# Masked attention with a two-layer network behind it: ten late hidden chunks computed as 2x2 blocks with seven block products

## The chip, the cores and the metric

The kernel runs on one core of a Trainium2 chip. Its engines are TensorE (PE; its weight loads are listed as PEld), VectorE (DVE), ScalarE (ACT), GpSimd (POOL) and SyncE (SP, which here issues all DMAs). The metric is device time in microseconds of one launch.

## The reference

Attention over 8 batches, 8 heads, 576 tokens and head size 64, in which only scores within `tau` of the row's maximum count, and then two dense layers on the 4608 tokens (512 features, 2048 hidden units):

```
scores = scale * q @ k^T
scores = where(scores >= max - tau, scores, -1e9)
x = softmax(scores) @ v            # (4608, 512) over all heads
h = x @ w_in                       # (4608, 2048)
g = max(h, 0) + alpha * min(h, 0)
out = g @ w_out                    # (4608, 512)
```

q, k and v are float32. The weights arrive as 64-bit floating point words and are decoded on the chip. Every float32 matrix operand is split into a high and a low part in the matmul format fp32r, and a product is the sum of three matmuls: high by high, high by low, low by high.

## The kernel before

The hidden units are 16 chunks of 128 (`fc`). The attention works on 32 pairs of heads, in cycles of nine units per pair; its finished outputs go to DRAM (`xs`, features by tokens). The first seven chunks (`F1 = 7`, the early chunks) are worked off as filler between the attention's matmuls: for groups of 256 tokens (`G1`), layer one (`pha`, L210) and layer two (`acca`, L246), and the sum over the early chunks is stored to DRAM as `part`. `Mlp.cycle` decides by a budget of TensorE time how much filler a cycle gets, and a group of tokens counts as ready only when its batch has left the attention. What is left of the early chunks when the attention ends is done behind it, under the names `phj` and `accj` with 256 columns.

Then come nine late chunks in two rounds, four and five chunks, each over all nine groups of 512 tokens (`G2`): x is loaded and split (`xhj` on ScalarE, `xlj` on GpSimd, L835 and L836), layer one takes 12 matmuls of 512 columns per chunk and group, VectorE makes the prelu (L228, L229), ScalarE and GpSimd split it (`gj`, L237 and L240), layer two takes three matmuls of 512 columns per chunk and block of 128 tokens (L246), and VectorE adds the stored partial sum (`pinj`, L988). Gates never leave the core. The weights of the late chunks are decoded piece by piece (128x512 words, class `Split64`: two operations on ScalarE, then on VectorE L137 clamp, L140 shift, L145 sign, L150 power, L156 rest) beside the matmuls of the round ahead.

Within each engine the instructions run in the order in which the program was written. `at_cycle(c, f)` puts a step into that order at a place counted in cycles; behind the attention a cycle is a place in the program, not a time. A tile whose tag has one buffer can be written again only when the last reader of its former content has finished.

## Time and profile before

| | us |
|---|---|
| median of 3 runs (lowest to highest) | 1376.98 (1376.14 to 1378.34) |
| span of the profiled execution | 1374.2 |
| TensorE busy | 1332.0 |
| VectorE busy | 989.5 |
| ScalarE busy | 843.4 |
| GpSimd busy | 825.4 |

The profiled execution's own time is known as its span, from the first to the last instruction; the three runs are other executions and lie 1.9 to 4.1 us above it. The last attention pair ends at about 833 us, the matmuls of the late chunks fill 931.6 to 1370.6 us, and the stretch between holds what is left of the early chunks. A row of an instruction group gives line, engine, operation, output and inputs, shapes and count, then busy time in us and the mean duration of one in ns, then idle time ahead of it and what ended that. A row of the timeline gives the start, the duration and the instruction.

### The profile page before, as it was taken

To read this page: it belongs to the slowest core of one execution; us is meant where nothing else is said; L and a number is where in the kernel's file an instruction comes from. 1 tells how busy PE (TensorE), PEld (TensorE's weight loads), DVE (VectorE), ACT (ScalarE), POOL (GpSimd) and SP (SyncE) were. 2 spreads that over 40 slices of the span, in tenths; PEclk is the share of its full clock that TensorE was granted. 3 is DMA by queue.
4 is the path that set the end of the run, shared out by engine and by line. 5 is a ranking of instruction groups with operands and counts; after the bars stand their busy time and mean duration, and the time that the engine had idled before them with its cause. 6 is when DMAs were issued, how large, how long until landed. Compare 5 with 4: busy or idle time off the path is not lost.

```text
span 1374.2 us, 24020 instructions
## 1 busy us (share of the span) xinstructions
PE 1332.0 (97%) x8116; PEld 1178.4 (86%) x8116; DVE 989.5 (72%) x1970; ACT 843.4 (61%) x1915; POOL 825.4 (60%) x949
## 2 busy tenths in 40 slices
PE   5988899999999999999999999999999999999998
PEld 4556789999999999999999998898888888888887
DVE  6999988889889889888888883873655644333432
ACT  6888888888888888888888873442323322211110
POOL 4886676576676666666666654884656554433431
PEclk9999999999999999999999999999999999999999
DMA  8643634644544545445445313445556352343222
GB/s 253 175 145 104 184 103 119 167 125 125 160 122 134 148 126 144 136 126 150 136 132 145 115 50 110 131 131 169 167 170 200 122 184 92 109 150 110 93 77 77
DMA packets 115179, 186.06 MB, mean 135 GB/s; under 512 B 18320, under 2 KB 49328, under 8 KB 115056
## 3 DMA queue, kind: packets, MB, share of 16 engines
q1 hardware_dynamic: 115056, 184.52, 45.0%
q8 instruction: 65, 1.06, 0.3%
q14 instruction: 58, 0.48, 0.1%
HBM read 104.41 MB, written 37.90 MB: 104 GB/s over the span
## 4 chain that ended last, share of the span: by engine, by line
PE 86%; ACT 5%; DVE 4%; issue 2%; POOL 2%; DMA 2%; SPq 0%; POOLq 0%; DVEq 0%; ACTq 0%
PE accj L246 19%; PE phj L210 18%; PE s L423 11%; PE av L570 11%; PE acca L246 9%; PE pha L210 9%; PE t L467 7%; PE tk L483 1%; DVE p L458 1%; DVE nmx L438 1%; DMA wri<-in_moe_w_in_dram 1%; ACT xb L583 1%; ACT p L446 1%; ACT xa L581 1%; ACT xh L196 1%
## 5 line engine op out<-in xcount | busy, mean ns | idle before, releaser
L240 POOL TENSOR_TENSOR gj<-ptj,gj 128x512 fp32r<-128x512 f32 (+1 forms) x109 | 129.2, 1187 | 237.2 <-ACT gj L237 236.5
L237 ACT ACTIVATE gj<-ptj 128x512 fp32r<-128x512 f32 (+1 forms) x109 | 62.9, 577 | 338.1 <-DVE ptj L229 338.0
L438 DVE TENSOR_REDUCE nmx<-s 128x1 f32<-128x576 f32 x288 | 217.2, 754 | 71.5 <-PE s L423 68.0
L246 PE MATMUL accj<-wo,gj 128*128 128x512 f32 x1140 | 262.4, 389 | 0.5 <-POOL gj L240 0.5
L246 PEld LDWEIGHTS accj<-wo,gj 128*128 128x128 f32 x1140 | 213.7, 188 | 45.3 <-POOL gj L240 1.0
L210 PE MATMUL phj<-xhj,wi 128*128 128x512 f32 (+1 forms) x816 | 232.7, 366 | 0.0
L458 DVE SCALAR_TENSOR_TENSOR p<-s,thr,p 128x576 f32<-128x576 f32 x256 | 206.9, 808 | 2.8 <-ACT thr L451 2.4
L446 ACT ACTIVATE p<-s,nmx 128x576 f32<-128x576 f32 x256 | 190.2, 743 | 8.2 <-DVE nmx L438 7.7
L246 PE MATMUL acca<-wo,ga 128*128 128x512 f32 x588 | 185.9, 422 | 1.6 <-POOL ga L240 0.8
L423 PE MATMUL s<-kh,qst 128*128 128x288 f32 x640 | 142.4, 313 | 33.6 <-DVE p L458 19.1
L210 PEld LDWEIGHTS phj<-xhj,wi 128*128 128x128 f32 x816 | 147.4, 188 | 25.4
L228 DVE TENSOR_SCALAR ptj<-phj,alpha_sb 128x512 f32<-128x512 f32 (+1 forms) x109 | 74.3, 681 | 124.1 <-PE phj L210 120.2
L210 PE MATMUL pha<-xh,wi 128*128 128x256 f32 x784 | 156.8, 283 | 0.2 <-ACT pra L223 0.2
L467 PE MATMUL t<-ident,p 128*128 128x128 f32 x1024 | 154.7, 274 | 0.0
L210 PE MATMUL phj<-xlj,wi 128*128 128x512 f32 (+1 forms) x408 | 149.8, 367 | 1.1 <-POOL xlj L836 0.9
L423 PEld LDWEIGHTS s<-kh,qst 128*128 128x128 f32 x640 | 101.4, 193 | 57.6 <-issue 25.1
L988 DVE TENSOR_TENSOR obj<-accj,pinj 128x512 f32<-128x512 f32 x72 | 49.8, 692 | 139.5 <-PE accj L246 118.5
L423 PE MATMUL s<-kl,qst 128*128 128x288 f32 x640 | 133.7, 299 | 0.0
L210 PEld LDWEIGHTS pha<-xh,wi 128*128 128x128 f32 x784 | 127.9, 190 | 4.5 <-ACT pra L223 1.5
L467 PEld LDWEIGHTS t<-ident,p 128*128 128x128 f32 x1024 | 126.5, 141 | 0.1
L233 POOL TENSOR_TENSOR pta<-pta,pra 128x256 f32<-128x256 f32 x94 | 69.4, 738 | 74.2 <-ACT pra L223 71.6
L246 PEld LDWEIGHTS acca<-wo,ga 128*128 128x128 f32 x588 | 102.0, 191 | 13.7 <-POOL ga L240 1.3
(130 smaller groups left out, 2867.3 us busy)
## 6 DMA issues: line engine op xcount, KB each, us to landing
pinj<-part SPq DMA_DIRECT2D x72, 256.0 KB
kr<-in_k_dram SPq DMA_DIRECT2D x31, 320.0 KB
rb<-rvd SPq DMA_DIRECT2D x64, 144.0 KB
xs<-xa SPq DMA_DIRECT2D x32, 288.0 KB
part<-obj SPq DMA_DIRECT2D x36, 256.0 KB
out_dram<-obj SPq DMA_DIRECT2D x36, 256.0 KB
vr<-in_v_dram SPq DMA_DIRECT2D x28, 320.0 KB
...
```

The source lines that it names most:

```text
L210: nc.tensor.matmul(ph[:, :n], w[:, c, :], xx[:, c, :n], start=(c == 0 and ti == 0), stop=(c == NCC - 1 and ti == 2),)
L228: nc.vector.tensor_scalar(t[:, :n], ph[:, :n], 0.0, alpha_sb[:, fc : fc + 1], op0=ALU.min, op1=ALU.mult)
L233: nc.gpsimd.tensor_tensor(t[:, :n], t[:, :n], r[:, :n], op=ALU.add)
L237: nc.scalar.activation(g[:, 0, :n], t[:, :n], AF.Copy)
L240: nc.gpsimd.tensor_tensor(g[:, 1, :n], t[:, :n], f(g[:, 0, :n]), op=ALU.subtract)
L246: nc.tensor.matmul(acc[:m, :], gg[:, g, o : o + m], w, start=(first and ti == 0), stop=(last and ti == 2))
L423: nc.tensor.matmul(ps[:, h, :288], w, kk[:, a + h * 288 : a + (h + 1) * 288], start=(ki == 0 and i == 0), stop=(ki == 1 and i == n - 1),)
L438: nc.vector.tensor_reduce(self.nmx[:, j : j + 1], self.S[u][0][:, :, :288], axis=AX.XY, op=ALU.max, negate=True)
L446: nc.scalar.activation(pj, ps[:, :, :288], AF.Exp, bias=nmx[:, j : j + 1], scale=1.0)
L458: nc.vector.scalar_tensor_tensor(pj, ps[:, :, :288], thr[:, j : j + 1], pj, op0=ALU.is_ge, op1=ALU.mult, accum_out=self.sm[:, c : c + 1])
L467: nc.tensor.transpose(tb[:, c, :], pt[:, j, j * D + c * P : j * D + (c + 1) * P], ident)
L570: nc.tensor.matmul(pa[:m, :n], w, x, start=(part == 0 and c == 0), stop=(part == z.parts[-1] and c == NKC))
```

## The change

The early chunks are six (`F1 = 6`), the late ones ten. The ten late chunks form five pairs. Both layers of a pair are computed on 2x2 blocks: a block product of eight becomes a set of seven, numbered 1 to 7, whose operands are sums and differences of blocks; the products of a set accumulate in three PSUM banks (`X` takes 1, 6, 5 and 3, `W` 7 and 4, `Y` 2).

- **Stage A**, the whole first layer of the late chunks: 6 blocks (`s`) of 768 tokens by 5 pairs of chunks, 30 units (`u`). A product is 6 matmuls of 384 columns. For each block x is loaded in four parts (`xr`), four sums are made (`xt` and in place) and seven operands are split (`xh`, `xl`, 128x768) by GpSimd, in the first block by VectorE in part. Behind the products, ScalarE copies banks (`c1`, `c7`, `c6`), VectorE and GpSimd add and make the prelu, and the gates go to DRAM (`gd`).
- **Stage B**, the whole second layer: 9 steps (`s`) of 512 tokens. A product is 30 matmuls of 256 columns. The gates are loaded again (`gr`), summed on VectorE (`gt` and in place), and split into `gh` (ScalarE) and `gl` (VectorE for products 7 and 5, GpSimd for the others), 128x1280 each; these lie in three slots, `r % 3`. VectorE adds the banks to the loaded `part` (`pin`), which is stored as the output.
- **Weights**: the ten pieces of `w_in` are decoded, summed and split (`wa`) in the stretch behind the attention, those of `w_out` decoded during stage A (`wo32`), and summed and split in its last block (`wb`).

The diff, cut to its core (the two rounds that go, `decode_part`, `load_pins` and the loop over `jobs` with `parts2`, are left out, and so are loads and pool bookkeeping):

```diff
 S = 576
 NKC = 4
-F1 = 7
+F1 = 6
 G1 = 256
+H1 = 384
 G2 = 512
 
 
...
+    NP = len(fcs2) // 2
+    NJ = 2 * NP
+    NA = NT // (2 * H1) * NP
+    NB = NT // G2
+    H2 = G2 // 2
+    ORDER = ((0, 1), (1, 5), (0, 7), (0, 2), (1, 3), (0, 6), (0, 4))
+    TURN = ((1, 5), (0, 1), (1, 3), (0, 7), (0, 2), (0, 6), (0, 4))
+    LAST = ((0, 1), (1, 5), (0, 7), (1, 3), (0, 6), (0, 2), (0, 5), (0, 4), (0, 3))
+    BANK = {1: "X", 6: "X", 5: "X", 3: "X", 7: "W", 4: "W", 2: "Y"}
+    USE = (1, 7, 2, 6, 4, 5, 3)
+    gd = [dram.tile([2, NP, P, H1], F32, name=f"gd{h}") for h in range(NT // H1)]
+
...
+    def split_hi(dst, src):
+        nc.scalar.activation(dst, src, AF.Copy)
+
+    def split_lo(eng, dst, src, hi):
+        eng.tensor_tensor(dst, src, f(hi), op=ALU.subtract)
...
+        def word_piece(io, fc):
+            src = (src_i if io == "i" else src_o)(fc)
+            return Split64(mem.ws, ("w0", 2), mem.ws, ("w1", 2), ENG2[(fc + (io == "o")) % 2], *src)
+
...
+            def temps():
+                for n in (7, 6):
+                    st[n] = mem.ws.tile([P, m], F32, tag=f"sum{n}", name=f"sum{n}_{pr}", bufs=1)
+                st[5], st[3] = blk(1, 0), blk(0, 1)
+                st[1], st[2], st[4] = blk(0, 0), blk(0, 1), blk(1, 1)
+                tt = nc.vector.tensor_tensor
+                tt(st[7], st[1], st[5], op=ALU.subtract)
+                tt(st[6], st[4], st[7], op=ALU.subtract)
+
+            def hi(n):
+                wsum[pr, n] = mem.wa.tile([P, 2, m], F32R, tag=f"wa{pr}_{n}", name=f"wa{pr}_{n}")
+                split_hi(wsum[pr, n][:, 0], st[n])
+
+            def lo(n, eng):
+                split_lo(eng, wsum[pr, n][:, 1], st[n], wsum[pr, n][:, 0])
+
+            def later_sums():
+                tt = nc.vector.tensor_tensor
+                tt(st[5], st[5], st[4], op=ALU.add)
+                tt(st[3], st[2], st[6], op=ALU.subtract)
+
+            at_cycle(c, temps)
...
+        def first_weights(c0, step):
+            for n, fc in enumerate(fcs2):
+                w = word_piece("i", fc)
+                c = c0 + step * n
+                at_cycle(c + 6, start_w32, fc)
+                word_at(c, w, None, c - 3)
...
+        p1.close()
+        mem.xr = pool(2, "xraw", "left")
+        mem.br = pool(3, "br", "right")
+        mem.pa = pool(4, "pa", "right")
+
+        start = {}
+        steps = []
+        c = i + 1
+        for n in range(NA + NB + 1):
+            for lag, prod in {NA: TURN, NA + NB - 1: LAST, NA + NB: ()}.get(n, ORDER):
+                u = n - lag
+                if 0 <= u < NA + NB:
+                    start[u, prod] = c
...
+        def x_at(s):
+            u = s * NP
+            st = {}
+            need = {n: start[u, n] for n in USE}
+            first = s == 0
+
+            def load():
...
+                        nc.sync.dma_start(r[:, :, t - t0 : t - t0 + m], src)
+                        t += m
+
+            tt = (nc.vector if first else nc.gpsimd).tensor_tensor
+
+            def temp(n):
+                st[n] = mem.xr.tile([P, 2, H1], F32, tag="xt", name=f"xt{s}_{n}", bufs=2)
+                return st[n]
+
...
+            def hi(n):
+                xop[s, n] = tuple(
+                    mem.pa.tile([P, 2, H1], F32R, tag=t, name=f"{t}{s}_{n}", bufs=7) for t in ("xh", "xl")
+                )
+                split_hi(xop[s, n][0], st[src(n)])
+
+            def lo(n):
+                split_lo(nc.vector if first and n in (7, 6) else nc.gpsimd, xop[s, n][1], st[src(n)], xop[s, n][0])
+
+            if first:
+                at = lambda c, fn, *a: fn(*a)
+            else:
+                at = at_cycle
+            at(need[1] - 20, load)
+            for n in USE:
+                c = need[n] - 6
+                fn = {7: sub7, 6: add6, 4: sub4, 5: sub5}.get(n)
+                if fn:
+                    at(c - 2, fn)
+                at(c, hi, n)
+                at(c + 1, lo, n)
+
+        x_at(0)
+        for put in puts:
+            put()
+        left[5].close()
+        ps_3 = left[5].enter_context(tc.tile_pool(name="ps_3", bufs=1, space=PSUM, reuse_waits="tile"))
+        for s in range(1, NA // NP):
...
+        def psum(u, prod):
+            b = BANK[prod]
+            fresh = prod in (1, 7, 2)
+            if fresh:
+                bank[u, b] = ps_3.tile([P, 512], F32, tag=b, name=f"p{b}{u}", bufs=3 if b == "X" else 2)
+            return bank[u, b], fresh
+
+        def product_a(u, prod):
+            s, pr = divmod(u, NP)
+            ph, fresh = psum(u, prod)
+            w = wsum[pr, prod]
+            xh, xl = xop[s, prod]
+            for c in range(2):
+                wh, wl = (w[:, k, c * P : (c + 1) * P] for k in range(2))
+                for ti, (a, x) in enumerate(((wh, xh), (wh, xl), (wl, xh))):
+                    nc.tensor.matmul(
+                        ph[:, :H1],
+                        a,
+                        x[:, c],
...
+        def after_a(u, prod):
+            s, pr = divmod(u, NP)
+            ph = bank[u, BANK[prod]][:, :H1]
+            if prod in (1, 7, 6):
+                t = sv[u, prod] = mem.br.tile([P, H1], F32, tag=f"c{prod}", name=f"c{prod}_{u}", bufs=2)
...
+            al = alpha_sb[:, fc : fc + 1]
+            t = mem.br.tile([P, H1], F32, tag="ct", name=f"ct{prod}_{u}", bufs=2)
+            if of is None:
+                g = mem.br.tile([P, H1], F32, tag="cr", name=f"cr{u}", bufs=1)
+                nc.vector.tensor_scalar(t, ph, 0.0, al, op0=ALU.min, op1=ALU.mult)
+                nc.scalar.activation(g, ph, AF.Relu)
+                nc.gpsimd.tensor_tensor(g, g, t, op=ALU.add)
+            else:
+                g = sv.pop((u, of))
+                nc.vector.tensor_tensor(g, ph, g, op=ALU.add)
+                nc.vector.tensor_scalar(t, g, 0.0, al, op0=ALU.min, op1=ALU.mult)
+                nc.vector.scalar_tensor_tensor(g, g, 0.0, t, op0=ALU.max, op1=ALU.add)
+            nc.sync.dma_start(gd[2 * s + k][r, pr], g)
+
+
...
+        for n in range(NJ):
+            c = begin + 8 + 12 * n
+            fc = fcs2[n]
+            word_at(c, word_piece("o", fc), wo32[:, n // 2, n % 2], c - 4)
+
+        bsum, gop, pin = {}, {}, {}
...
+        def gates_at(s):
+            u = NA + s
+            need = {n: start[u, n] for n in USE}
+            use = sorted(USE, key=need.get)
...
+            def temp(n):
+                st[n] = mem.b1.tile([P, NP, H2], F32, tag="t", name=f"gt{s}_{n}", bufs=2)
+                return st[n]
+
+            def sub7():
+                tt(temp(7), st[0, 0], st[1, 0], op=ALU.subtract)
+
...
+            src = lambda n: {1: (0, 0), 2: (0, 1), 4: (1, 1)}.get(n, n)
+
+            def hi(n):
+                r = 7 * s + use.index(n)
+                home = mem.b2 if r % 3 == 2 else mem.b1
+                gop[s, n] = tuple(
+                    home.tile([P, NP, H2], F32R, tag=f"{t}{r % 3}", name=f"{t}{s}_{n}") for t in ("gh", "gl")
+                )
+                split_hi(gop[s, n][0], st[src(n)])
+
+            def lo(n):
+                split_lo(nc.vector if n in (7, 5) else nc.gpsimd, gop[s, n][1], st[src(n)], gop[s, n][0])
+
+            for k, (h, j) in enumerate(((0, 0), (1, 0), (0, 1), (1, 1))):
+                at_cycle(max(need[1] - 16 + k, turn + 1 if s == 0 else start[NA - 1, 3] + 1), load, h, j)
+            at_cycle(need[1] - 8, load_pins)
+            for n in USE:
+                c = need[n] - 6
+                if s == 0 and n == 2:
+                    c = start[NA - 1, 3] + 1
+                fn = {7: sub7, 6: sub6, 5: add5, 3: sub3}.get(n)
+                if fn:
+                    at_cycle(c - 2, fn)
...
+        def product_b(u, prod):
+            acc, fresh = psum(u, prod)
+            s = u - NA
+            gh, gl = gop[s, prod]
+            todo = [(tb, pr) for tb in range(2) for pr in range(NP)]
+            for n, (tb, pr) in enumerate(todo):
+                wh, wl = (bsum[pr, prod][:, k] for k in range(2))
+                for ti, (g, w) in enumerate(((gh, wh), (gh, wl), (gl, wh))):
...
+        def after_b(u, prod):
+            s = u - NA
+            acc = bank[u, BANK[prod]].rearrange("p (a m) -> p a m", a=2)
+            h, k = {1: (0, 0), 2: (0, 0), 6: (1, 0), 4: (1, 0), 7: (1, 1), 5: (1, 1), 3: (0, 1)}[prod]
+            dst = pin[s, h][:, :, k * H2 : (k + 1) * H2]
+            nc.vector.tensor_tensor(dst, acc, dst, op=ALU.add)
+            if prod == (3 if h == 0 else 4 if start[u, 4] > start[u, 5] else 5):
+                t0 = G2 * s + H2 * h
+                nc.sync.dma_start(out[t0 : t0 + H2, :].rearrange("(a p) m -> p a m", p=P), pin[s, h])
...
+        for u, prod in steps:
+            assert i <= start[u, prod], (u, prod, i, start[u, prod])
+            while i < start[u, prod]:
+                if i == turn:
+                    turn_over()
+                cycle()
+            (product_a if u < NA else product_b)(u, prod)
+            if (u, prod) == (NA - 1, 3):
+                turn_again()
+            at_cycle(i + 1, after_a if u < NA else after_b, u, prod)
+        for _ in range(3):
+            cycle()
+    for st in reversed(left):
         st.close()
 
 
```

Three places show how instructions move. The first is ScalarE behind the attention. Before, in the rounds of nine chunks, it splits x and the prelu:

```order
L237 ACTIVATE gj_8_14468<-ptj_8_14465 128x512
L237 ACTIVATE gj_9_14490<-ptj_9_14487 128x512
L237 ACTIVATE gj_10_14510<-ptj_10_14507 128x512
L237 ACTIVATE gj_7_14538<-ptj_7_14535 128x512
L835 ACTIVATE xhj_14575<-xrj_0_14527 128x512
L835 ACTIVATE xhj_14575<-xrj_1_14529 128x512
```

Now, in stage B, it writes the high parts; the name is `gh`, the step, and the product, and the brackets name the engines and queues whose semaphores a row waits on:

```order
L842 ACTIVATE gh1_1_15769<-gr1_00_15680 128x1280 [waits DMAHW0_49,PE_49,Pool_49]
L842 ACTIVATE gh0_5_15805<-gr0_10_15382 128x1280 [waits DVE_49]
L842 ACTIVATE gh1_7_15843<-gt1_7_15819 128x1280 [waits DVE_49,PE_49,Activation_49]
L842 ACTIVATE gh1_2_15878<-gr1_01_15684 128x1280 [waits DMAHW2_49]
L842 ACTIVATE gh0_3_15918<-gr0_01_15400 128x1280 [waits DVE_49,PE_49,Pool_49]
L842 ACTIVATE gh1_6_15964<-gt1_6_15935 128x1280 [waits DVE_49]
L842 ACTIVATE gh1_4_15999<-gr1_11_15686 128x1280 [waits DMAHW3_49]
L842 ACTIVATE gh2_1_16038<-gr2_00_15902 128x1280 [waits PE_49,Pool_49]
```

Three of a step's seven rows, 1, 7 and 3, now wait on TensorE (PE): they take the slot of the product that stands one place ahead in `ORDER`.

The second place is GpSimd. Before, in the rounds of nine chunks, its low parts are spread between those of the prelu:

```order
L240 TENSOR_TENSOR gj_7_13976<-ptj_7_13973,gj_7_13976 128x512
L156 TENSOR_TENSOR wti_13896<-wti_13896,wi_13993 128x512
L836 TENSOR_TENSOR xlj_14014<-xrj_0_13961,xhj_14013 128x512
L836 TENSOR_TENSOR xlj_14014<-xrj_1_13964,xhj_14013 128x512
L156 TENSOR_TENSOR wi_13993<-wti_13896,wri_13773 128x512
L836 TENSOR_TENSOR xlj_14014<-xrj_2_13967,xhj_14013 128x512
```

Now, in stage A, a block of 768 tokens brings one run of eleven; `cr` is a gate of a unit before:

```order
L1134 TENSOR_TENSOR xt_7_13293<-xr_11_13127,xr_01_13129 128x768
L845 TENSOR_TENSOR xl_1_13291<-xr_00_13125,xh_1_13290 128x768
L845 TENSOR_TENSOR xl_7_13320<-xt_7_13293,xh_7_13319 128x768
L1141 TENSOR_TENSOR xt_6_13334<-xt_7_13293,xr_00_13125 128x768
L845 TENSOR_TENSOR xl_2_13332<-xr_10_13131,xh_2_13331 128x768
L1144 TENSOR_TENSOR xt_4_13348<-xr_10_13131,xt_6_13334 128x768
L1221 TENSOR_TENSOR cr_13351<-cr_13351,ct_3_13350 128x384
L845 TENSOR_TENSOR xl_6_13363<-xt_6_13334,xh_6_13362 128x768
L1138 TENSOR_TENSOR xr_01_13129<-xr_01_13129,xr_00_13125 128x768
L845 TENSOR_TENSOR xl_4_13379<-xt_4_13348,xh_4_13378 128x768
L845 TENSOR_TENSOR xl_5_13406<-xr_01_13129,xh_5_13405 128x768
```

The seventh low part follows behind one more `cr`. All of these move into about two units' length of products.

The third place is VectorE in the stretch behind the attention, while the early chunks end. Before, one decoding operation stands between two prelus:

```order
L229 SCALAR_TENSOR_TENSOR ptj_4_12718<-phj_4_12704,ptj_4_12718 128x256
L145 SCALAR_TENSOR_TENSOR wti_12672<-wri_12591,wti_12672 128x512
L228 TENSOR_SCALAR ptj_5_12738<-phj_5_12724,alpha_sb 128x256
L229 SCALAR_TENSOR_TENSOR ptj_5_12738<-phj_5_12724,ptj_5_12738 128x256
L150 TENSOR_SCALAR wri_12591<-wti_12672 128x512
L228 TENSOR_SCALAR ptj_6_12760<-phj_6_12744,alpha_sb 128x256
```

Now two pieces are decoded side by side, and their sums (`w`, `sum`) and low parts (`wa`) stand between as well:

```order
L981 TENSOR_TENSOR w_6_12281<-w_6_12281,sum_0_12370 128x256
L146 SCALAR_TENSOR_TENSOR wti_12358<-wri_12287,wti_12358 128x512
L151 TENSOR_SCALAR wri_12287<-wti_12358 128x512
L138 TENSOR_SCALAR wti_12413<-wti_12413 128x512
L845 TENSOR_TENSOR wa_3_12432<-w_6_12281,wa_3_12432 128x256
L830 TENSOR_TENSOR wri_12287<-wri_12287 128x512
L141 TENSOR_SCALAR wti_12413<-wti_12413 128x512
L1002 TENSOR_TENSOR w_9_12463<-wti_12358,wri_12287 128x512
L146 SCALAR_TENSOR_TENSOR wti_12413<-wri_12361,wti_12413 128x512
L229 TENSOR_SCALAR ptj_1_12471<-phj_1_12450,alpha_sb 128x256
L230 SCALAR_TENSOR_TENSOR ptj_1_12471<-phj_1_12450,ptj_1_12471 128x256
```

Nine operations now stand ahead of this prelu where one stood, and the first operand of stage A stands behind the last of them.

More of the change, by code (lines that the diff above doesn't have):

```diff
@@ L987, in second_layer @@
-                ob = mem.mp1.tile([P, DM], F32, tag="ob", name=f"ob{job.name}_{o}", bufs=3)
-                nc.vector.tensor_tensor(ob[:m], acc[:m], job.pins[o][:m], op=ALU.add)
-                dst = out[job.t0 + o : job.t0 + o + m, :] if job.last == len(parts2) - 1 else part[gi][r : r + m, :]
-                nc.sync.dma_start(dst, ob[:m])
-        mem.gb = GB
+                    nc.sync.dma_start(part[job.gi][o : o + m, :], po[:m])
+                puts.append(put)
+                if pool is mem.mp1:
+                    puts.pop()()
@@ new lines, in product_a @@
+        def product_a(u, prod):
[10 more added lines that the diff above has]
+                        x[:, c],
+                        start=(fresh and c == 0 and ti == 0),
+                        stop=(c == 1 and ti == 2),
+                        skip_group_check=not fresh,
+                    )
@@ new lines, in turn_over, with turn_again @@
+        def turn_over():
+            left[2].close()
+            left[1].close()
+            mem.b1 = pool(1, "b1", "left")
+        def turn_again():
+            left[4].close()
+            mem.b2 = pool(4, "b2", "right")
+        turn = start[NA - NP, 3] - 3
+        for pr in range(NP):
+            weights_b(pr)
+        for s in range(NB):
+            gates_at(s)
+        for u, prod in steps:
[8 more added lines that the diff above has]
+            at_cycle(i + 1, after_a if u < NA else after_b, u, prod)
```

221 lines of the change are left out of this document (165 added, 56 removed).

## The prediction

> **What bounds the kernel now.** I read the page first, its busy shares and the chain of waits, then the windows by stage, and last the rows of single instructions.
>
> ```profile
> span 1374.2 us, 24020 instructions
> PE 1332.0 (97%) x8116; PEld 1178.4 (86%) x8116; DVE 989.5 (72%) x1970; ACT 843.4 (61%) x1915; POOL 825.4 (60%) x949
> ...
> PE 86%; ACT 5%; DVE 4%; issue 2%; POOL 2%; DMA 2%; SPq 0%; POOLq 0%; DVEq 0%; ACTq 0%
> ```
>
> TensorE is busy 97% and holds 86% of the chain. The windows (columns: stretch and length, then PE, PEld, DVE, ACT, POOL busy with counts, clock, DMA share, GB/s) say whether that holds in each stage: a pair with little filler, two steady pairs, the rest of the first chunks, the nine late chunks.
>
> ```profile
> 147.80:171.50 23.70, 21.03 (x160) 19.78 (x158) 22.10 (x50) 21.68 (x53) 16.92 (x20) 1.00 0.62 169
> 553.00:603.80 50.80, 50.72 (x374) 48.37 (x372) 44.94 (x100) 44.04 (x105) 33.58 (x43) 1.00 0.47 136
> 851.80:915.20 63.40, 62.28 (x408) 56.68 (x407) 55.97 (x87) 30.88 (x67) 50.65 (x49) 1.00 0.42 130
> 931.60:1370.60 439.00, 438.43 (x1933) 362.34 (x1931) 196.06 (x286) 101.58 (x175) 208.18 (x159) 1.00 0.41 132
> ```
>
> In the last 439 us TensorE has no gap; VectorE and GpSimd are under half busy. In the rest of the first chunks VectorE is at 88% and GpSimd at 80%: little cover is left there.
>
> **TensorE's arithmetic.** Matmuls overlap, so a price is the distance between starts.
>
> ```profile
> 850.09 0.28 PE L210 MATMUL phj<-xl,wi 128*128 128x256 f32 x1
> 850.45 0.28 PE L210 MATMUL phj<-xl,wi 128*128 128x256 f32 x1
> ...
> 875.13 0.28 PE L210 MATMUL phj<-xlj,wi 128*128 128x256 f32 x1
> 875.48 0.28 PE L210 MATMUL phj<-xlj,wi 128*128 128x256 f32 x1
> ...
> 942.51 11.04 PE L246 MATMUL accj<-wo,gj 128*128 128x512 f32 x48
> 953.39 0.39 PE L210 MATMUL phj<-xhj,wi 128*128 128x512 f32 x1
> ```
>
> Three matmuls of 256 columns take 0.35 to 0.36, so 0.118 each (0.117 to 0.120); 48 of 512 take 10.88, 0.2267 each. No row has 384 columns; between the two, 0.1724. Removed: one early chunk, 216 of 256 columns (25.5) and 108 of 512 (24.5), and the nine late chunks, 1944 of 512 (440.7). Added: stage A, 30 units of 7 products of 6 matmuls, 1260 x 0.1724 = 217.2; stage B, 9 steps of 7 products of 30, 1890 x 0.118 = 223.0. Net **-50.5** (-44 to -54). Seven for eight is nearly eaten by the shorter matmuls: ten late chunks cost 440.2, as nine did. What is gained is the early chunk.
>
> **Attention.** Of that, 17.3 us of filler leave the pairs, 15.9 of it in six (10, 11, 14, 15, 18, 19), 2 to 3.2 each: with six chunks, filler runs out before the next tokens are ready. The row that marks the end of a pair gives the rhythm:
>
> ```profile
> 147.80 0.27 PE L593 MATMUL rp<-ident,rv 128*9 128x128 f32 x1
> 171.51 0.27 PE L593 MATMUL rp<-ident,rv 128*9 128x128 f32 x1
> ...
> 780.90 0.27 PE L593 MATMUL rp<-ident,rv 128*9 128x128 f32 x1
> 806.14 0.27 PE L593 MATMUL rp<-ident,rv 128*9 128x128 f32 x1
> ```
>
> A full pair takes 25.2, one with TensorE only 21.03 of 23.7 busy still 23.7, with VectorE at 93%. So a pair can shrink by 1.5, six by 9: **+8** of the 17.3 are not had (0 to 16).
>
> **Stage B, the largest term.** Each product needs a high part (ScalarE, 128x1280) and a low part (GpSimd, or VectorE for 7 and 5). They sit in three slots, `r % 3`, r = 7s + place in 1,7,2,6,4,5,3. The products run as 1, 5 of the step before, 7, 2, 3 of the step before, 6, 4. The slots along that order, with a = 7s mod 3, are a, a+1, a+1, a+2, a+2, a, a+1, and the next step begins with a+1. Three times a step a product has its predecessor's slot: 7 behind 5, 2 ahead of 3, 4 ahead of the next 1. ScalarE may not write the slot until TensorE has finished the predecessor; TensorE has nothing else in its order.
>
> ```profile
> L196 ACT ACTIVATE xh<-xr 128x1024 fp32r<-128x1024 f32 x15 | 15.9, 1058 | 0.2
> L350 ACT ACTIVATE kh<-kr 128x640 fp32r<-128x640 f32 x31 | 22.9, 738 | 0.6
> ...
> L198 POOL TENSOR_TENSOR xl<-xr,xh 128x1024 fp32r<-128x1024 f32 x15 | 35.8, 2387 | 13.3 <-ACT xh L196 13.3
> ...
> L341 DVE TENSOR_TENSOR kl<-kr,kh 128x640 fp32r<-128x640 f32 x1 | 0.8, 825 | 0.0
> L523 DVE TENSOR_TENSOR eo<-t,eo 128x512 fp32r<-128x512 f32 x112 | 76.7, 685 | 8.2 <-ACT eo L519 8.0
> L523 DVE TENSOR_TENSOR eo<-t,eo 128x256 fp32r<-128x256 f32 x56 | 20.6, 406 | 0.0
> ```
>
> No row has 1280 elements. ScalarE's two give 0.83 ns an element: 1.27. GpSimd at 2.33 ns: 2.98. VectorE at 1.09: 1.52. The hand-overs come from one chain at the end of the kernel:
>
> ```profile
> 1357.81 0.63 ACT L237 ACTIVATE gj<-ptj 128x512 fp32r<-128x512 f32 x1 [2.09 <-DVE ptj L229]
> 1358.52 1.27 POOL L240 TENSOR_TENSOR gj<-ptj,gj 128x512 fp32r<-128x512 f32 x1 [1.43 <-ACT gj L237]
> 1359.85 0.96 PE L246 MATMUL accj<-wo,gj 128*128 128x512 f32 x3 [0.54 <-POOL gj L240]
> ```
>
> ACT to POOL 0.08, POOL to PE 0.06; I take 0.11 from PE to ACT. A 256-column matmul's record runs 0.28 - 0.118 = 0.16 past its successor's place. A pause with GpSimd is then 0.16 + 0.11 + 1.27 + 0.08 + 2.98 + 0.06, less 0.24 for the two matmuls that need the high part alone: 4.42. With VectorE: 2.96. After the first step there are 8 of 7 behind 5, 8 of 1 behind 4, 7 of 3 behind 2 and, in the last order, one of 6 behind 3: 8 x 2.96 + 16 x 4.42 = **+94** (80 if GpSimd works at 1.9 ns, 110 at 2.8). Behind ScalarE's waiting copy for 7 stand those for 2 and 3, and on GpSimd 2's low part: 1.27 + 2.98 behind 7's, under 7's own 1.52 + 3.3, so it is not late, and 6's and 4's parts follow in the same way. On VectorE the sum for 3 and the adds from PSUM stand behind 7's low part, with the 3.5 us of product 2 to spare. So the pauses are the whole loss.
>
> **The rest of the first chunks.** The ten W_in pieces are now decoded, summed and split behind 18 instead of 28 group-chunk products. These rows show what VectorE's SBUF-only work costs beside GpSimd's (minimum, median, maximum of a line first):
>
> ```profile
> L137 DVE TENSOR_SCALAR wto<-wto x16: 412/786/1410, 61.1 to 1098.4; 128x512 f32<-128x512 f32 x16
> L145 DVE SCALAR_TENSOR_TENSOR wto<-wro,wto x16: 679/963/1866, 68.1 to 1103.8; 128x512 int32<-128x512 int32 x16
> L156 DVE TENSOR_TENSOR wri<-wri x9: 682/686/1115, 857.6 to 1028.5; 128x512 f32<-128x512 f32 x9
> ...
> 907.32 1.40 DVE L140 TENSOR_SCALAR wto<-wto 128x512 int32<-128x512 int32 x1
> 908.76 1.66 DVE L145 SCALAR_TENSOR_TENSOR wto<-wro,wto 128x512 int32<-128x512 int32 x1
> ...
> 906.92 1.52 POOL L156 TENSOR_TENSOR wto<-wto,wo 128x512 f32<-128x512 f32 x1
> ...
> L228 DVE TENSOR_SCALAR ptj<-phj,alpha_sb 128x256 f32<-128x256 f32 x21 | 10.0, 478 | 4.9 <-PE phj L210 3.1 <-POOL gj L240 1.3 <-POOL xlj L836 0.6
> L229 DVE SCALAR_TENSOR_TENSOR ptj<-phj,ptj 128x256 f32<-128x256 f32 x22 | 9.3, 425 | 0.8
> ...
> L228 DVE TENSOR_SCALAR ptj<-phj,alpha_sb 128x512 f32<-128x512 f32 x81 | 60.9, 751 | 108.4 <-PE phj L210 108.2
> ```
>
> VectorE's 1.40 at 907.32 ends 0.28 behind GpSimd's (906.92 + 1.52): it waited for it. In 851.8 to 915.2 VectorE's 55.97 hold 19.3 of prelu, which reads PSUM and keeps its price; the other 44 took 36.7. Alone they are 24 x 0.42, 8 x 0.68 and 12 x 0.68 = 23.7: a factor of 1.55. In the change VectorE has 18 x 0.90 = 16.2 of prelu, and 30 x 0.42, 10 x 0.68, 15 x 0.68 and 34 halves at 0.42 = 43.9, by 1.55 68: 84. TensorE has 25.5 + 24.5 there, and VectorE starts some 3 ahead; the first product of A needs the last piece, and its own operands another 4. 84 - 53 + 4 = 35; GpSimd is less dense over the longer time, so I take **+30** (11 at no factor, 41 at 1.69).
>
> **Stage A.** A unit is 7.24 us of matmuls. VectorE's share: three adds of 384 from PSUM at 0.55 (between the L523 rows), one PSUM operation at 0.61 (between L228's 0.48 for 256 and 0.75 for 512 columns), three at 0.35 and three at 0.55 within SBUF: 2.25 + 2.7 x 1.55 = 6.4. W_out's pieces, 2.96 alone every 12 products, add 1.73 x 1.55 = 2.7 for 17 units: 9.1 against 7.24, 32 in all. W_out's sums and low parts in the last five units add 7 x 0.42 x 1.55 = 4.6: 11.0, another 19. GpSimd makes a block's four sums and seven low parts, 11 x 1.79 (768 elements at 2.33), within some 14 products: where VectorE doesn't set the pace, 6's and 4's low parts come 3 to 4 late. For two blocks 9. Together **+60** (18 with no interference, five late bursts; 100 if each burst lets VectorE do one SBUF operation per GpSimd operation). What I cost at nothing: ScalarE's copies (7 x 0.85 and 20 x 0.5 in a block of 36 us), and DMA. SP issues 20 gate stores a block, which wait for VectorE or GpSimd, and ahead of the next block's x loads in its order; those are placed 20 products early, so a store some us late delays nothing. 3.9 MB of gates and 1.6 of x in 36 us are 153 GB/s, and the first window above moved 169. Without that cover a load's lateness would be the next block's start.
>
> Entry into B and the last, larger store: +4. **Sum:** 1374.2 - 50.5 + 8 + 94 + 30 + 60 + 4 = 1519.7. The profiled execution has a span of 1374.2, the median of the runs shown is 1376.98, 2.8 more: 1522; I say **1520**.
>
> **Rivals.** (1) *TensorE stays gap-free; faster.* The parts come in time and VectorE keeps up: 1374.2 - 50.5 + 8 + 4 + 2.8 = 1338. For it: ScalarE and GpSimd are idle half of the last stage now. Against: the slot is given up only at its reader's end. It decides if pauses, rest and A together stay under 38. 4%. (2) *Little interference:* rest +10, A +18, B as forecast: 1460. For it: in the last 439 us L137 often runs at 0.42; against: GpSimd was idle there more than half the time. 20%. (3) *Strict turns:* rest +41, A +100, B +102: 1580. For it the rows at 907; 13%. (4) *The clock falls in the pauses.* The longest wait of TensorE after its start is 2.1 us:
>
> ```profile
> PE s L423 <- DVE p L458: 19.1, 22, 2.1
> ```
>
> Nothing here shows the clock after longer ones. If each pause were followed by as long a time at half clock, 94/2 = 47 more: 1567. 10%. The Trainium skill (TensorE: Matmul & The Clock Gate, HAM oscillation — how this bites in real kernels) warns of idle gaps over about 3.4 us, after which the array runs at half clock; by it the pauses of 4.4, broken by two matmuls, are at the edge, and no run here shows it. The forecast keeps 53%.
>
> **Range and chances.** 1460 to 1585 holds the forecast, (2), (3) and most of (4). A difference of 0.2% is about what a measurement of this kernel tells from none; all cases but (1) lie far above. Faster 3%, same 1%, slower 96%.
>
> **What would show it.** Right: TensorE's waits on ScalarE's `gh` and GpSimd's `gl` lead the waits, some 24 pauses, stage B 315 to 325 long; VectorE's `wa` rows and its prelu rows within SBUF at 1.5 times their bare price, and A 270 to 290 long. Wrong: gap-free matmuls in B, A near 217, or a 384-column matmul far from 0.172.

## The result and the profile after

The change takes 1653.77 us (median of 4 runs, 1652.39 to 1653.91) against 1377.36 for the kernel before on the same chip (median of 4): a ratio of 1.2011, interval 1.1994 to 1.2028. It is slower, as forecast, but by 276 us where 143 were forecast, and it lies 69 us above the range.

The page of the change: its length, busy shares, the granted clock in 40 slices and the shares of the chain of waits.

```profile
span 1652.1 us, 26173 instructions
PE 1395.0 (84%) x8998; PEld 1287.9 (78%) x8998; DVE 1228.5 (74%) x2203; ACT 917.4 (56%) x2019; POOL 884.8 (54%) x910
...
PEclk9998999999999999999988778999999788888889
...
PE 57%; DVE 13%; issue 11%; ACT 8%; POOL 7%; DMA 4%; SPq 1%; ACTq 0%; POOLq 0%; DVEq 0%
```

TensorE falls from 97% to 84% busy and from 86% to 57% of the chain. The digits of the clock, 9 nearly everywhere in the attention, are 7 and 8 in most slices behind it. So TensorE loses time twice: it stands still, and part of the time in which it is "busy" it runs slowly.

The windows of the change for the rest of the early chunks, stage A and stage B (stretch, length, busy time of PE, PEld, DVE, ACT and POOL with counts, clock, DMA share, GB/s), and the end of the last attention pair:

```profile
851.60:962.40 110.80, 66.91 (x324) 54.80 (x325) 75.99 (x126) 36.21 (x90) 49.28 (x54) 0.77 0.30 95
962.40:1288.30 325.90, 247.57 (x1256) 235.27 (x1256) 283.30 (x391) 108.68 (x216) 173.53 (x114) 0.91 0.37 123
1288.30:1652.10 363.80, 277.24 (x1897) 267.06 (x1896) 149.52 (x123) 75.29 (x65) 132.97 (x47) 0.87 0.34 107
```
```profile
837.41 0.27 PE L594 MATMUL rp<-ident,rv 128*9 128x128 f32 x1
```

Against the stages as the forecast's terms make them:

| | forecast | measured | miss |
|---|---|---|---|
| end of the attention | 833.4 - 17.3 + 8 = 824.1 | 837.4 | +13 |
| rest of the early chunks | 25.5 + 24.5 + 30 = 80 | 110.8 | +31 |
| stage A | 217.2 + 60 = 277 | 325.9 | +49 |
| stage B and the end | 223.0 + 94 + 4 = 321 | 363.8 | +43 |

The span of 1652.1 exceeds the forecast's 1519.7 by 132; the four misses make 135.6, and the stretch between attention and rest gives 3 back.

TensorE's waits of the change, stage B first, then stage A, then ScalarE's longest in the rest (engine and line <- what ended the wait: us, times, longest):

```profile
PE pX L1353 <- POOL gl L845: 39.5, 16, 2.5
PE pX L1353 <- ACT gh L842: 20.7, 16, 1.3
PE pW L1353 <- ACT gh L842: 10.3, 8, 1.3
PE pW L1353 <- DVE gl L845: 8.2, 8, 1.0
PE pY L1353 <- POOL gl L845: 3.0, 1, 3.0
```
```profile
PE pX L1195 <- ACT c L1211: 54.8, 18, 8.2
PE pX L1195 <- DVE c L1224: 21.7, 14, 3.7
```
```profile
ACT wti L134 <- DMA wri<-in_moe_w_in_dram: 50.0, 9, 6.8
```

Stage B shows the pauses of the forecast to the count: 16 behind GpSimd, 8 behind VectorE, and the entry. One of them in the timeline of TensorE (start, duration, instruction, idle time ahead), with the matmuls behind it:

```profile
1407.37 0.28 PE L1353 MATMUL pX<-wb,gl 128*128 128x256 f32 x1
1408.94 0.50 PE L1353 MATMUL pW<-wb,gh 128*128 128x256 f32 x2 [1.29 <-ACT gh L842]
1410.47 0.58 PE L1353 MATMUL pW<-wb,gl 128*128 128x256 f32 x1 [1.03 <-DVE gl L845]
1410.85 0.63 PE L1353 MATMUL pW<-wb,gh 128*128 128x256 f32 x2
1411.28 0.41 PE L1353 MATMUL pW<-wb,gl 128*128 128x256 f32 x1
...
1413.76 0.28 PE L1353 MATMUL pW<-wb,gl 128*128 128x256 f32 x1
...
1414.12 0.28 PE L1353 MATMUL pW<-wb,gl 128*128 128x256 f32 x1
```

From 1410.85 to 1411.28 two matmuls take 0.43, 0.21 each; from 1413.76 to 1414.12 three take 0.36. For 3 us behind the pause TensorE runs at half its speed. Counted over all rows (a matmul is slow where the next start lies over 1.3 times the full-clock distance away with no wait between, and only the time beyond that distance is counted), stage B loses 81.8 us to waits and 43 to the half clock, stage A 78 and 24, the rest 45 and 14. The half clock alone is 81 us. Ahead of each wait the record of the last matmul also runs about 0.16 us past its successor's place, 8 us in B and 6 in A; the 51 and 29 in the expectations below count this with the half clock.

### The profile page after: what moved, and what is told of

Read it like the earlier page. It is cut to its first block, busy times and chain, and to the rows that moved or that the text cites. A ratio compares the mean times of both kernels' runs of the same rounds, so it can differ in the third digit from the quotient of the medians.

```text
span 1652.1 us, 26173 instructions
## 1 busy us (share of the span) xinstructions
PE 1395.0 (84%) x8998; PEld 1287.9 (78%) x8998; DVE 1228.5 (74%) x2203; ACT 917.4 (56%) x2019; POOL 884.8 (54%) x910
## 4 chain that ended last, share of the span: by engine, by line
PE 57%; DVE 13%; issue 11%; ACT 8%; POOL 7%; DMA 4%; SPq 1%; ACTq 0%; POOLq 0%; DVEq 0%
PE av L571 10%; PE s L424 9%; PE acca L247 7%; PE pX L1353 7%; PE pha L211 7%; PE t L468 6%; POOL gl L845 4%; PE pX L1195 3%; PE pW L1353 3%; DVE ct L1225 3%; DMA wri<-in_moe_w_in_dram 2%; PE pY L1353 2%; DVE c L1224 2%; PE pW L1195 1%; ACT gh L842 1%
## 5 line engine op out<-in xcount | busy, mean ns | idle before, releaser
L845 POOL TENSOR_TENSOR gl<-gr,gh 128x1280 fp32r<-128x1280 f32 x36 | 108.2, 3007 | 205.5 <-ACT gh L842 205.5
L1195 PE MATMUL pX<-xh,wa 128*128 128x384 f32 x480 | 147.9, 364 | 76.5 <-ACT c L1211 54.8
L1353 PE MATMUL pX<-wb,gh 128*128 128x256 f32 x720 | 157.2, 319 | 20.7 <-ACT gh L842 20.7
L1195 PEld LDWEIGHTS pX<-xh,wa 128*128 128x128 f32 x480 | 94.8, 202 | 88.2 <-ACT c L1211 61.3
L842 ACT ACTIVATE gh<-gr 128x1280 fp32r<-128x1280 f32 x45 | 55.9, 1262 | 179.0 <-issue 77.4
L1353 PEld LDWEIGHTS pX<-wb,gh 128*128 128x128 f32 x720 | 133.6, 227 | 23.9 <-ACT gh L842 23.9
L1353 PE MATMUL pX<-wb,gl 128*128 128x256 f32 x360 | 115.9, 322 | 39.5 <-POOL gl L845 39.5
L1353 PEld LDWEIGHTS pX<-wb,gl 128*128 128x128 f32 x360 | 82.0, 228 | 42.8 <-POOL gl L845 42.8
L571 PE MATMUL av<-eo,vst 128*128 128x322 f32 (+1 forms) x512 | 107.8, 334 | 0.0
L424 PEld LDWEIGHTS s<-kl,qst 128*128 128x128 f32 x640 | 104.1, 194 | 0.0
```

Of the source, the lines that this page charges most:

```text
L424: nc.tensor.matmul(ps[:, h, :288], w, kk[:, a + h * 288 : a + (h + 1) * 288], start=(ki == 0 and i == 0), stop=(ki == 1 and i == n - 1),)
L571: nc.tensor.matmul(pa[:m, :n], w, x, start=(part == 0 and c == 0), stop=(part == z.parts[-1] and c == NKC))
L842: nc.scalar.activation(dst, src, AF.Copy)
L845: eng.tensor_tensor(dst, src, f(hi), op=ALU.subtract)
L1195: nc.tensor.matmul(ph[:, :H1], a, x[:, c], start=(fresh and c == 0 and ti == 0), stop=(c == 1 and ti == 2), skip_group_check=not fresh,)
L1353: nc.tensor.matmul(acc[:, tb * H2 : (tb + 1) * H2], g[:, pr, tb * P : (tb + 1) * P], w, start=(fresh and n == 0 and ti == 0), stop=(n == l ...
```

## The experiments

Theory: four separate losses, namely shared slots in B with the half clock they bring; VectorE held up by GpSimd in A; ScalarE's queue in A behind a relu that waits for VectorE; the weight loads in the rest. The rivals stand with each run. All times are medians of 4 runs; ratios are to the kernel before, measured beside it.

**Slots by order of execution** (`e1_ring`).

```diff
+        rank = {step: n for n, step in enumerate(t for t in steps if t[0] >= NA)}
...
-                r = 7 * s + use.index(n)
+                r = rank[u, n]
```

> One edit in stage B: the slot of gh and gl is the rank of the product in the order in which TensorE runs the products of B, modulo 3, so no product has its predecessor's slot. Against 1653.8 us of the change. Theory (the 25 double pauses, 82 us idle, come from the shared slots, and the 51 us of matmuls at half clock from the pauses): both go but for the entry, 1520 to 1540, granted clock of B from 0.87 to 0.98 or more. Rival 1 (the clock falls in B for a reason of its own): only the idle time goes, about 1575, clock of B still under 0.9. Rival 2 (GpSimd and VectorE cannot prepare seven operands in a step of 25 us, and the slots only hide it): the pauses move and stay, 1620 or more, TensorE still waits for gl over 40 us.

Measured: 1525.59 us, ratio 1.1072 (1.1051 to 1.1093), 128 us less than the change. Its window of stage B and TensorE's only wait there:

```profile
1285.60:1523.60 238.00, 229.22 (x1897) 228.81 (x1896) 125.75 (x123) 79.16 (x65) 153.13 (x47) 0.98 0.51 164
```
```profile
PE pY L1354 <- POOL gl L845: 3.0, 1, 3.0
```

The stage falls from 363.8 to 238.0, the clock rises from 0.87 to 0.98, and slow matmuls cost 3 us instead of 43. The theory holds; both rivals fall. The same parts, made by the same engines (GpSimd busy 153 of 238), come in time once the slots follow the order of use.

**Short pauses only** (`e10_short_pauses`). To see what a pause itself does to the clock, one shared slot per step is left, that of 7 behind 5.

```diff
-                r = 7 * s + use.index(n)
+                r = {1: 0, 5: 1, 7: 1, 2: 2, 3: 0, 6: 1, 4: 2}[n]
```

> Stage B with a slot for each product (1, 3: 0; 5, 7, 6: 1; 2, 4: 2) in place of the counter, so that of the three shared slots per step only that of 7 behind 5 is left: 8 pauses in two parts, 1.29 and 1.03 us, with two matmuls between. Everything else as in the change; to be held against slots by order of execution (1525.6). Theory (a pause of 2.3 us of idle time is enough for a stretch of about 3.5 us at half clock behind it): 8 x (2.74 + 1.8) = 36, and a few in the last step, whose order differs: 1560 to 1570, with matmuls 0.21 apart behind each of the 8. Rival (the clock falls only for the pauses of 4.2 us and those that come shortly after them; a pause under 3.4 us costs its own length alone): 8 x 2.74 = 22, 1545 to 1552, matmuls 0.12 apart behind them.

Measured: 1566.61 us, ratio 1.1383 (1.1364 to 1.1403). TensorE's longest waits for GpSimd in B, and from the timeline the end of one pause, which has the same two parts as in the change:

```profile
PE pX L1353 <- POOL gl L845: 6.3, 5, 1.6
PE pY L1353 <- POOL gl L845: 5.3, 1, 5.3
```
```profile
1409.88 0.38 PE L1353 MATMUL pW<-wb,gl 128*128 128x256 f32 x1 [1.03 <-DVE gl L845]
```

The time is the theory's, but in part by luck: waits for GpSimd's parts, which neither side had counted, make some 10 us of it. The rows decide better. Of the 8 pauses, 5 were followed by 2.9 to 4.4 us of slow matmuls, 3 by none. So 2.3 us of idle time are enough, though not each time, and the rival's "never" is wrong.

What decides can be read from the windows. The granted clock of this trace changes only every 3.41 us, on one grid that runs through it. Here are two neighbouring stretches of that grid around the pause above, then two around a pause that was followed by no slow matmuls (columns as in the windows above):

```profile
1407.01:1410.42 3.41, 1.09 (x7) 0.83 (x7) 2.08 (x3) 2.43 (x2) 0.88 (x1) 1.00 0.00 0
1410.42:1413.83 3.41, 3.41 (x18) 3.41 (x17) 3.41 (x2) 0.00 (x0) 2.20 (x1) 0.50 0.02 5
```
```profile
1434.31:1437.72 3.41, 2.44 (x21) 2.24 (x19) 0.00 (x0) 1.00 (x1) 0.00 (x0) 1.00 0.56 185
1437.73:1441.14 3.41, 2.07 (x15) 1.87 (x16) 3.12 (x3) 1.42 (x2) 1.91 (x1) 1.00 0.00 0
```

The first pause falls into one stretch and leaves TensorE 1.09 us busy in it; the next stretch runs at half clock, from 1410.42, half a microsecond after the pause has ended at 1409.88. The second pause is shared by two stretches, which keep 2.44 and 2.07 us busy, and the clock stays. So it is with all eight: each of the five has a stretch in which TensorE is busy for 53% or less, the three others have none under 55%.

**Relu first** (`e2_relu_first`).

```diff
+                nc.scalar.activation(g, ph, AF.Relu)
                 nc.vector.tensor_scalar(t, ph, 0.0, al, op0=ALU.min, op1=ALU.mult)
-                nc.scalar.activation(g, ph, AF.Relu)
```

> One edit in stage A: ScalarE's relu of product 3's bank is written ahead of VectorE's min-times-alpha of the same bank, so ScalarE waits for TensorE and not for VectorE's queue. Against 1653.8. Theory (the bank copies c come late because they stand behind the waiting relu in ScalarE's queue): TensorE's 54.8 us of waits for c in A go for the most part, with half of the 29 us at half clock: 1585 to 1610. Rival (VectorE is the bound of A, held up by GpSimd while it makes the next block's operands): the wait changes its name to VectorE's c, A loses under 15 us: 1638 or more.

Measured: 1640.43 us, ratio 1.1912 (1.1894 to 1.1929): 13 less, the rival's result. TensorE's waits in A:

```profile
PE pX L1195 <- DVE c L1224: 41.3, 18, 5.4
PE pX L1195 <- ACT c L1211: 19.5, 6, 6.3
```

The wait changed its name: 54.8 + 21.7 became 19.5 + 41.3. ScalarE's copies had come late because VectorE was late.

**No x work behind the first block** (`e6_no_x`), on top of relu first.

```diff
         for s in range(1, NA // NP):
-            x_at(s)
+            for n in USE:
+                xop[s, n] = xop[0, n]
```

> On top of the relu put first (1640.4 us): blocks 1 to 5 of stage A use the split operands of block 0, so their x loads, sums, high and low parts are left out (five times 11 operations of about 2 us on GpSimd and 7 of 0.84 on ScalarE). VectorE's and TensorE's work in A stays whole. Theory (A's loss is VectorE held up by GpSimd): VectorE's second and third step of the prelu come back to about 0.42 and 0.56 us in blocks 1 to 5, A goes from 316 to 240 to 260 us, 1565 to 1585. Rival (VectorE's own work, W_out's decoding included, overloads A): under 20 us gained, 1620 or more.

Measured: 1573.95 us, ratio 1.1422 (1.1403 to 1.1441), 66 less than relu first; A takes 246 us for 312. Two groups of VectorE, relu first in all of A, then this run in the blocks without x work (line, engine, operation, tiles, shapes, count, busy us, mean ns, idle ahead):

```profile
L1226 DVE SCALAR_TENSOR_TENSOR c<-c,ct 128x384 f32<-128x384 f32 x88 | 89.2, 1013 | 3.0
L1225 DVE TENSOR_SCALAR ct<-c,alpha_sb 128x384 f32<-128x384 f32 x88 | 67.2, 763 | 5.1
```
```profile
L1227 DVE SCALAR_TENSOR_TENSOR c<-c,ct 128x384 f32<-128x384 f32 x68 | 40.0, 588 | 2.3
L1226 DVE TENSOR_SCALAR ct<-c,alpha_sb 128x384 f32<-128x384 f32 x68 | 35.1, 516 | 4.1
```

VectorE's operations are the same; GpSimd's x work is gone (busy 66 us of A instead of 177), and the mean falls from 1013 to 588 ns. The x loads and 35 of ScalarE's high parts are gone too, so the 66 us alone do not show that GpSimd is the cause; the rows of VectorE do. How one holds up the other is seen in the timelines of the change, VectorE above, GpSimd below:

```profile
1112.54 2.10 DVE L1226 SCALAR_TENSOR_TENSOR c<-c,ct 128x384 f32<-128x384 f32 x1
1114.56 2.31 DVE L830 TENSOR_TENSOR wro<-wro 128x512 f32<-128x512 f32 x1
1116.79 0.54 DVE L1224 TENSOR_TENSOR c<-pX,c 128x384 f32<-128x384 f32 x1
```
```profile
1112.25 1.97 POOL L1134 TENSOR_TENSOR xt<-xr,xr 128x768 f32<-128x768 f32 x1
1114.18 2.14 POOL L845 TENSOR_TENSOR xl<-xr,xh 128x768 fp32r<-128x768 f32 x1
```

VectorE's first row ends at 1114.64, 0.42 behind GpSimd's end at 1114.22; its second at 1116.87, 0.55 behind the end at 1116.32. They take turns, one for one. L1224, which reads PSUM, keeps its 0.54, though GpSimd starts another operation within it, at 1116.95.

**Sum and prelu in PSUM** (`e5_psum_prelu`), on top of relu first.

```diff
-                nc.vector.tensor_tensor(g, ph, g, op=ALU.add)
-                nc.vector.tensor_scalar(t, g, 0.0, al, op0=ALU.min, op1=ALU.mult)
-                nc.vector.scalar_tensor_tensor(g, g, 0.0, t, op0=ALU.max, op1=ALU.add)
+                z = g if prod == 5 else ph
+                nc.vector.tensor_tensor(z, ph, g, op=ALU.add)
+                nc.vector.tensor_scalar(t, z, 0.0, al, op0=ALU.min, op1=ALU.mult)
+                nc.vector.scalar_tensor_tensor(g, z, 0.0, t, op0=ALU.max, op1=ALU.add)
```

> On top of the relu put first (1640.4 us, stage A about 316 us): in stage A the sum and the prelu of products 2 and 4 stay in their PSUM bank until the last operation, so four of VectorE's six operations within SBUF per unit read PSUM instead. Bare, that is more work for VectorE (0.61 for 0.42 and about 0.6 for 0.56, some 0.4 us a unit, 12 us in all). Theory (VectorE's operations that read SBUF alone wait for the end of GpSimd's running operation, those that read PSUM don't, and this sets A): the waits of VectorE shrink in the 22 us of GpSimd's work per block, A 280 to 300, 1605 to 1625. Rival (VectorE is simply overloaded by its own work): 1645 to 1660.

Measured: 1628.6 us, ratio 1.1818 (1.1794 to 1.1843): 12 less than relu first, 4 over the theory's upper end and well below the rival. VectorE's groups in A:

```profile
L1227 DVE SCALAR_TENSOR_TENSOR c<-c,ct 128x384 f32<-128x384 f32 x29 | 32.0, 1104 | 1.0
...
L1227 DVE SCALAR_TENSOR_TENSOR c<-pY,ct 128x384 f32<-128x384 f32 x30 | 16.7, 558 | 1.0
```

The same operation takes 558 ns where one operand lies in PSUM and 1104 where all lie in SBUF. The gain is small although VectorE is busy 257 us of A instead of 287. The third that stayed in SBUF now takes longer (1104 for 1013 ns, 885 for 763), and the wait moves: TensorE's waits behind VectorE's `c` fall from 41.3 to 18.4 us, those behind ScalarE's copies rise from 19.7 to 30.9.

**x's sums and low parts on VectorE** (`e8_x_vector`), on top of relu first: work moved onto the busier engine.

```diff
-            tt = (nc.vector if first else nc.gpsimd).tensor_tensor
+            tt = nc.vector.tensor_tensor
...
-                split_lo(nc.vector if first and n in (7, 6) else nc.gpsimd, xop[s, n][1], st[src(n)], xop[s, n][0])
+                split_lo(nc.vector if not first or n in (7, 6) else nc.gpsimd, xop[s, n][1], st[src(n)], xop[s, n][0])
```

> On top of the relu put first (1640.4 us, A 312 us, VectorE busy 287 of them, 156 in 176 prelu operations within SBUF that would take some 87 alone): the sums and low parts of x in blocks 1 to 5 go from GpSimd to VectorE, which is the busier engine. Nothing is left out. Theory (an operation of VectorE within SBUF and one of GpSimd exclude each other, so each of GpSimd's 2 us costs VectorE's queue more than the 0.9 us that VectorE needs for the same work): the prelu operations go back to about 0.52 and 0.59 as in the run without x work, VectorE needs 265 to 280 in A and sets its length: A 280 to 295, 1610 to 1625. Rival (VectorE is merely overloaded, whoever shares the SBUF): the 50 us of x work come on top of 287, A 340 to 360, 1670 to 1690.

Measured: 1618.31 us, ratio 1.1749 (1.1724 to 1.1775): 22 less, as the theory had it. VectorE has 55 operations more in A and is busy 267 us instead of 287; the prelu's two groups are down to 608 and 499 ns:

```profile
L1226 DVE SCALAR_TENSOR_TENSOR c<-c,ct 128x384 f32<-128x384 f32 x88 | 53.5, 608 | 3.0
L1225 DVE TENSOR_SCALAR ct<-c,alpha_sb 128x384 f32<-128x384 f32 x88 | 43.9, 499 | 5.1
L845 DVE TENSOR_TENSOR xl<-xr,xh 128x768 fp32r<-128x768 f32 x20 | 19.0, 951 | 0.0
```

A low part that held GpSimd for 2 us costs VectorE 0.95. The Trainium skill (SBUF — State Buffer, SBUF: two separate sides) states this mechanism: the two engines share a port pair that one of them holds for a whole instruction while the other is fully blocked. The rows above agree, the free PSUM readers included.

**Early loads** (`e3_early_loads`).

```diff
-            return Split64(mem.ws, ("w0", 2), mem.ws, ("w1", 2), ENG2[(fc + (io == "o")) % 2], *src)
+            return Split64(mem.ws, ("w0", 3), mem.ws, ("w1", 2), ENG2[(fc + (io == "o")) % 2], *src)
...
-                word_at(c, w, None, c - 3)
+                word_at(c, w, None, max(i, c - 6))
...
-            xr = st["xr"][k] = mem.lx.tile([P, G1], F32, tag="xr", name=f"xr{name}_{k}", bufs=NCC)
+            xr = st["xr"][k] = mem.lx.tile([P, G1], F32, tag="xr", name=f"xr{name}_{k}", bufs=NCC - 1)
```

> One edit in the stretch behind the attention: three raw buffers for the weight pieces instead of two, and the load six cycles ahead of the decode instead of three (one of the four small x buffers is given up for the space). Against 1653.8. Theory (every second piece is a serial chain of load, decode, load, and ScalarE's and VectorE's queues stand behind the waiting piece): the stretch of 112 us shrinks to 80 to 90, 1620 to 1632. Rival (VectorE's decode, sums and splits, 76 us busy of these 112, set its length, with GpSimd's interference): ScalarE's wait for the load falls, but the stretch loses under 8 us: 1645 or more.

Measured: 1630.52 us, ratio 1.1845 (1.1823 to 1.1866): 23 less. In the change, SP issued the first two loads of the rest together and the next two only when the first pieces' buffers came free, at 871.50 and 880.43:

```profile
851.95 0.38 SPq L124 DMA_DIRECT2D wri<-in_moe_w_in_dram  x1
...
852.93 0.42 SPq L124 DMA_DIRECT2D wri<-in_moe_w_in_dram  x1
...
871.50 9.31 SPq L124 DMA_DIRECT2D wri<-in_moe_w_in_dram  x2
```

With three buffers ScalarE's wait for these loads falls from 50.0 to 2.7 us and the stretch is 86.6 long; for another 16 us ScalarE now waits until a piece's other buffer is free:

```profile
ACT wti L134 <- DMA wri<-in_moe_w_in_dram: 2.7, 1, 2.7
```

**Six early chunks alone** (`e4_six_early`), from the kernel before.

```diff
-F1 = 7
+F1 = 6
...
-DEC2, DEC3 = 5, 6
+DEC2, DEC3 = 3, 6
```

> The kernel before with six early chunks and ten late ones (five and five) in its own ordinary products, and the late pieces decoded every 3 cycles instead of every 5 so that they come in time: the chunk count alone. The late rounds are then 48.97 us of matmuls longer and the rest of the early chunks 33 to 50 us of matmuls shorter. Theory (the attention gives nothing back for the filler that leaves it, and the stretch behind it is set by the decoding of ten pieces and not by TensorE): attention ends at 833 to 838 as in the change, the rest takes 60 us or more, 1400 to 1425. Rival (what the change lost ahead of stage A comes from its own code alone, its sums and buffers): 1377 to 1395.

Measured: 1416.83 us, ratio 1.0285 (1.0268 to 1.0303). The attention ends at 834.7, 1.3 us later than with seven; then (windows up to the first matmuls of layer one with 512 columns, and from them):

```profile
834.70:910.70 76.00, 61.27 (x352) 53.34 (x350) 57.33 (x82) 32.39 (x69) 49.83 (x50) 0.89 0.48 150
910.70:1414.80 504.10, 498.79 (x2196) 411.55 (x2194) 223.66 (x322) 113.59 (x198) 233.72 (x181) 1.00 0.38 120
```

The kernel before reaches these at 919.3, ahead of the 931.6 at which its window of the late chunks begins. So an early chunk less (50.0 us of matmuls) brings 9 us ahead of the late rounds, and a late chunk more costs 49 in them: the chunk count alone costs 39 us, before any block product (with the faster decoding, every 3 cycles, that goes with it here). Against this, the block products save 49 us of matmuls, 489.7 for ten chunks in ordinary products against 440.2.

**Together.** Slots, relu first, early loads and the PSUM prelu (`e7_all`); and the first three with x on VectorE in place of the PSUM prelu (`e9_x_vector_all`). Their diffs are those above.

> The four edits together: slots by order of execution, relu first, three raw buffers with early loads, sum and prelu of products 2 and 4 in PSUM. If the losses are separate places and add up: 1653.8 less 128, 13, 23 and what the PSUM prelu brings (20 to 35): 1455 to 1470. If one stands behind the other (time gained in one stage is lost again to loads or parts that are late in the next): 1480 or more. Either way it stays over the kernel before, since VectorE's bound in A and behind the attention is still there.

> Slots by order of execution, relu first, early loads with three raw buffers, and x's sums and low parts on VectorE. The gains so far added up without a loss (128.2, 13.4, 23.3, and the PSUM prelu's 11.8 gave 176.6 together). If x on VectorE brings 20 and adds up too: about 1469. If VectorE, now without slack in A, meets the high and low parts of the next stage late: 1480 to 1500.

Measured: 1477.24, ratio 1.0727 (1.0699 to 1.0754), and 1465.92, ratio 1.0644 (1.0622 to 1.0666). For the first, the single gains of 128.2, 13.3, 23.3 and 11.8 are 176.6 and the run has 176.5: they add up. It lies above the 1455 to 1470 expected for it, because the PSUM prelu had been put in at 20 to 35. The second comes within 3 us of its 1469. The losses are separate places, and the best version found is still 89 us behind the kernel before. The largest gap left is in A, 291 us long for 218 of matmuls.

## Why the prediction fell short

**Arithmetic: right.** Six matmuls of 384 columns lie between these two starts of the change:

```profile
1109.76 0.34 PE L1195 MATMUL pW<-xh,wa 128*128 128x384 f32 x1
...
1110.80 0.34 PE L1195 MATMUL pX<-xh,wa 128*128 128x384 f32 x1
```

That is 0.1733 each, where 0.1724 had been interpolated. The matmuls themselves are as short as forecast.

**The pauses of stage B: right.** 24 and the entry. A pause with VectorE costs 2.74 (1407.37 to 1410.47 for what would be 0.36), with GpSimd 4.19, for 2.96 and 4.42: 89 us for the 94. (The bounds that stand beside the 94, 80 and 110, come to 86 and 104 by the same terms.)

**The clock: the step that failed.** "(4) The clock falls in the pauses" was a rival at 10%; the forecast kept full speed. It priced the fall at 47 in stage B, and 40 came there behind the pauses (43 less the 3 inside them). But it was looked for only in B: A's gaps and the rest's brought another 24 and 14. That is 78 of the 132 us by which the span missed the forecast. In B the clock is shown to follow the pauses (`e1_ring`); in A, where VectorE holds TensorE up, the 24 are an account and not what a full clock would gain.

The trace of before had shown a fall once. Its longest wait, the 2.1 us of the prediction, ends at 190.53, and these are its windows around it:

```profile
188.38:191.79 3.41, 1.34 (x11) 1.29 (x11) 3.02 (x8) 3.26 (x6) 2.31 (x3) 1.00 0.82 228
191.80:195.20 3.40, 3.40 (x18) 3.40 (x17) 1.84 (x5) 2.33 (x6) 3.20 (x3) 0.50 0.36 83
```

So a wait half as long as the pauses forecast for B was followed by 3.4 us at half clock. The forecast did not look there, and with this row 10% was low. The Trainium skill's rule (TensorE: Matmul & The Clock Gate, HAM oscillation — how this bites in real kernels) was another warning, and its 3.4 us were taken as a threshold that pauses broken by two matmuls might not cross. Here 2.3 us often sufficed.

**The rest: a cost put at nothing.** 80 us were forecast and 110.8 came. DMA was costed at nothing, weighed by GB/s over a block of A. What mattered was the order: two raw buffers, each held from the load to the end of the decoding, and a load only three cycles ahead. With three buffers and earlier loads the stretch takes 86.6, so the term of +30 was about right in length. Its factor was too high: VectorE was busy 76 us and not 84, which by the forecast's own bare prices is a factor of about 1.35.

**Stage A: the mechanism right, its size wrong.** +60 was forecast, 109 came, 24 of it slow matmuls. The 85 others were to come mainly from a factor of 1.55 on 0.55 us (L1226) and 0.35 (L1225): 0.85 and 0.54. The groups of VectorE in A of the change:

```profile
L1226 DVE SCALAR_TENSOR_TENSOR c<-c,ct 128x384 f32<-128x384 f32 x88 | 86.7, 985 | 3.0
L1225 DVE TENSOR_SCALAR ct<-c,alpha_sb 128x384 f32<-128x384 f32 x89 | 71.4, 802 | 5.2
```

The shortest of them take 557 and 419 ns, so the bare 0.35 was already too low. Even without x work (`e6_no_x`) they took 588 and 516 ns. The factor came from a stretch where GpSimd's operations are shorter (50.65 us for 49, 1.03 each) and have gaps; in A one operation of 2 us holds up one of VectorE's. That is rival (3), strict turns. ScalarE's relu, waiting for VectorE at the head of its queue, added 13 that the forecast had not seen: ScalarE was taken to be idle enough, but what stands behind a waiting instruction waits with it.

**The attention: +8 of 17.3 forecast, all 17.3 and 4 more measured.** With ordinary late rounds it is the same within 3 us (`e4_six_early`), so it lies in the chunk count. That pairs can shrink by 1.5 us was a bound from one row, not a rate; what left them came back elsewhere: TensorE's waits up to the last pair rose from 35.0 to 45.1 us, and the granted clock there fell from 0.998 to 0.986. The last 3 us lie within the spread: six runs that differ from the change only behind the attention reach its end at 832.1 to 837.4.

**The range** failed because the rivals were treated as excluding each other. (3) gave 1580; (4) on top of it 1627; the 24 us of the load chain make 1651. Each was named or could be, but the range was drawn up to the one or the other. That this sum comes so near is in part luck: (3) put 102 on B, where the pauses made 89, and the sum leaves out the clock in A and the rest.
